# Moving the last wide-quarter products of a fused RWKV6 and MLP kernel into the kv burst

## The chip, the cores and the metric

The kernel runs on one core of a Trainium2 chip. The metric is the device time of one execution in microseconds (us). In the profile TensorE is PE (its weight loads PEld), VectorE is DVE, ScalarE is ACT, GpSimd is POOL and SyncE is SP. "L708" is line 708 of the kernel's source.

## The reference

Attention in the RWKV6 manner runs over 4 batches, 8 heads, 768 tokens and 48 channels; its result, 3072 tokens of 384 channels, goes through an MLP with an exact gelu.

```
for t in range(S):
    cur = einsum('bhd,bhe->bhde', u * k_t, v_t)
    y[:, :, t] = einsum('bhd,bhde->bhe', r_t, state + cur)
    state = w_t[..., None] * state + einsum('bhd,bhe->bhde', k_t, v_t)
x = y.transpose(0, 2, 1, 3).reshape(3072, 384)
h = x @ w_in                      # 384 x 2048
g = 0.5 * h * (1 + erf(h / sqrt(2)))
out = g @ w_out                   # 2048 x 384
```

## The kernel before, in words

The 3072 tokens are cut into 8 tiles of 384: tile x is one half of one batch's sequence, so odd tiles continue from the state that the tile before left. Within a tile the tokens form chunks of 64. Attention in a tile is computed by chunks: scores between the tokens of a chunk, the chunk's contribution k^T v to the state ("kv"), the chain of states from chunk to chunk, then outputs from inside the chunk and from the state before it.

**Order of work.** The work is written as generators, and one instruction stream per engine comes from stepping them in an order that a string fixes. `PLAN[x]` is the string of stage x: in it the MLP of tile x-1 and attention of tile x (and the start of that of tile x+1) are interleaved. Each character steps one stream: "." a group of MLP products on PE, "s" and "f" attention of this and the following tile, "x" sums that the MLP takes of its input (L1036), "v" merges of products (additions on DVE or by POOL transfers, L1115 to L1120), "g" gelus (L1133), "o" sums for and of the output products (L1161 to L1167), "e" copies of accumulators (L1084), "l" loads, and in the first stages "c", "w", "y", "p" for converting the weights and summing them. Nothing reorders this later: an engine runs its instructions in program order, each waiting for those that it depends on.

**The MLP.** Both products use fast multiplication: 20 products of half-blocks each, with sums and merges of inputs and outputs around them on DVE, ACT and POOL. Nearly all PE records of the MLP come from one line (L1040), each 128x128 weights by 192 columns, 0.1625 us apart.

**Attention of tiles 2 to 7** (`quarters()`, lines 661 to 782) makes the scores of a chunk in two levels: quarters of 4 tokens (FINE) and quarters of 16 ("wide"). For each level the 12 blocks of chunks are cut at 0, 5, 10 and 12. For each part `burst()` runs 64x64 products on PE (L708) into a pair of PSUM banks called d; there are two such pairs, and kv_ps and y_ps come from the same pool. Then `copy_quarters()` copies the scores into a_sb: on DVE under masks for the fine level (L737), on ACT in six copies for the wide level (L724, in `copy_rows`). The third part's burst therefore waits until the first part's copies have freed a pair. After the bursts DVE scales r and k for the next level (L753, L760, L764); at the wide level it transposes k in 32x32 blocks (L657), and 12 transfers on SP's queue (L652) and four ACT copies (L806) put the blocks of k^T in place.

Then, for the tile as a whole:

- kv burst on PE, 96 records into two pairs kv_ps, b = 0 and 1 (L822)
- chain of states on DVE, `chain_states()`: 20 multiply-adds (L837), and on even tiles two copies (L842) ahead of them
- `inside()`: 96 products within the chunks into two pairs y_ps (L863)
- `fences()`: a DVE copy of two columns of each y_ps pair (L875), which reads them and which the next products therefore have to wait for
- products with the states, added onto y_ps (L908)
- ACT copies of y_ps to the MLP's input xT (L931, L934) and six SP transfers (L938)

`halves()` does the same for tiles 0 and 1 with other levels. The planner's string decides which MLP products stand between these steps: in tiles 4 and 6 one group of them stood between `inside()` and the products with the states.

Of the kernel before, what the change touches and what calls it, by code (L numbers as in the profile page):

```python
# [10 lines left out]
F32 = mybir.dt.float32  # L11
# [10 lines left out]
C = 64  # L22
G = 64
D = 48
T = 384
# [3 lines left out]
NI = Q * N3  # L29
# [9 lines left out]
PLAN = {  # L39
    0: "l.s....llsl.lssslslss.lc.l.slslls...ssss..lcs.s.s.l.ss..ss..sccs.c.s.llpssslw..cs.ffpccxx",  # L40
    1: (
        "l.ccswccclss.cw.l.ccccccscs.c.csscccc.scc.sscwccc.cswcs.wcsccscccls.c.ssc.sclcswcwcc.wcwcc"
        "sslcw..cwlclwccswclsc.cf.w.cw..ccc.cfw..cfyx....f.x..x.f.yxxf.wxw..y..y...wywyx..xyxf.yw.f"
        ".wxywxyl.yf."
    ),
    2: (
        "s.w..s.w.w.s..w..wswv.w..v.ww.vwv.ssw.swgww.swgsvwv.w.sgwv.wssls..wvsw...wg...g...wvsw.gvl"
        "s..sgvss...gg.ssvgvw.wvgvgvv.glsgv..gs.og.l.oe.s.wsoeo.s...seooe..l.so.ooe.lewo...o..ooeoe"
        "..os.eolol.s.se..oo.oew.lsw.ooosles..f.fo.oo.o.fo..xooxxfxxxxxfxfxx"
    ),  # L50
    3: (
        ".ls....v..s.sl...g...s.vvs..s..l.vg.gvg....s..l..sv.svss.ssss.g.svssgvlvg.sg..vv.vv.gsv.gv"
        "s.sggv.gslsvs..g.ogsog.e..s.eoo.....seo.oe.os.eoo.e...oooso.e.e.s.soo.ool.lessseo..oeolssf"
        "....fooo.e..f.xooxo.o..x.oooxlxxxfxfxfxx"
    ),
    4: (
        "ls.....s.ss.v....g....vlv.s.gs.vv..g....sv...s.glssvvgsvslsss..gvs.v.gs.ggss..v.sgv.vv..vv"
        ".slsggs.svsg.gog.g.s.oss.eo.e.o..o.so..ee..ooo..eoe.o..oosee.s..loo.os.oes.e.so.llsleo.of."
        "s.o.esolo.f..f.ooo.o.foo..xoxxxxxxxffxfxx"
    ),  # L60
    5: (
        ".....sll....v....vv..vsg.vs....ggs.v..vs.ls..g.sv.ssssvs.sl..g.vs.vsvgs.s.ggv.gss..l..vsvv"
        "vsssvg...ggsggogsg.os.oe.se.l.o..o..o.oe.es.o.oeeo....o..ooseoes..ose.loos.ssell..oo.eossf"
        "..o..fo.oeof..o..xoo.oxox.oxxlxxxffxfxx"
    ),
    6: (
        "s..sl...v.....v..g..ss.v.lvv...g.gvs..gsv..s.v..s.ssggsssvss..ss.l.vg.s..vg.vvggss..vvvv.."
        "ssssvggg..g.so.ggsoe...seo...ssols.o.o.eooe...o.e.eo.o.o.e.ooeo..ssl.oos.lsel..eslooo..lef"
        "s..oes.o.lfo..foo.o.o..fooxoxxxxxffxxxfxx"
    ),  # L70
    7: (
        "....sv.......gss.v....vsv..g..sg..vvg..s...s.svsgvsvss.ss.ss.vvgs.v.gsg.vg..svg...vv.ssgsv"
        "v.gg.g.sgso.gseo..es.....osso..ooo.eeoo..e.eso...oooee...os.soe..oos.se.s.oeosos...oo.e..."
        "oooo..oxo.oxx.oxxxxxxxx"
    ),
    8: (
        "..........v...v...v.v..g.gggv.v.....vv.....g.gvg....vgv.vvvgvgv..vgg..g.vgo..gge..eo...o.o"
        ".oo.eoe....oeo.e.o..o.oeeo..oo.eo.o.eo....ooe..o.e.oo.o..o.oo.oo.o"
    ),
}  # L80

# [111 lines left out]
def kernel(  # L193
# [9 lines left out]
    nc = tc.nc  # L203
# [13 lines left out]
    wk = ctx.enter_context(tc.tile_pool(name="wk", bufs=2))  # L217
# [7 lines left out]
    def pair(name):  # L225
        return pools["d"].tile([128, 2, BANK], F32, name=name, tag="d")
# [22 lines left out]
    half = [slice(0, 64), slice(64, 128)]  # L249
# [8 lines left out]
    bufs = [io.tile([128, 3 * NP * T], F32, name=f"rkw{i}", bufs=1) for i in range(2)]  # L258
# [218 lines left out]
    def attention(x, unit):  # L477

        first = x % HALVES == 0
        parts = range(NPART) if units_of(x) == 1 else range(unit, unit + 1)  # L480
        np_ = len(parts)
# [179 lines left out]
        def quarters():  # L661
# [28 lines left out]
            for h in QUARTERS:  # L690
                m, r4, t4, s0, s1, s2 = views(h)

                def burst(first, behind):

                    d = pair("d")
                    if behind == n_b and h == FINE:
                        for a in range(FINE):
                            for g in range(2):
                                for p in range(2):
                                    nc.tensor.matmul(fine_of(d, g)[half[p], a * n_b:],  # L700
                                                     lhsT=places[half[g], a, p * C:(p + 1) * C],
                                                     rhs=fine_sb[half[g], 0:FINE - a, a],
                                                     start=(a == 0), stop=True, skip_group_check=True)
                    for n in range(first, behind):
                        i = n - first
                        for g in range(2):
                            for p in range(2):
                                nc.tensor.matmul(d[half[p], g, i * 3 * C // 2:(i + 1) * 3 * C // 2],  # L708
                                                 lhsT=kc[half[g], n // NI, n % NI, p],
                                                 rhs=rx[half[g], 2 * n + p], start=True, stop=True,  # L710
                                                 skip_group_check=True)
                    return d
# [27 lines left out]
                last = h == QUARTERS[-1]  # L740
# [75 lines left out]
        kvs = []  # L816
        for b in range(np_):
            kv_ps = pair("kv_ps")
            for i in range(NI):
                for p in range(2):  # L820
                    for g in range(2):
                        nc.tensor.matmul(kv_ps[half[g], p, i * D:(i + 1) * D], lhsT=k_t(b, i, p, g),  # L822
                                         rhs=vs(b, i, g)[half[p], 0:D], start=True, stop=True)
# [28 lines left out]
        def inside():  # L852

            for b in range(np_):
                if split:
                    y = [bank("y_ps") for _ in range(2)]
                else:
                    y_ps = pair("y_ps")
                    y = [y_ps[:, c] for c in range(2)]
                for i in range(NI):  # L860
                    for p in range(2):
                        for g in range(2):
                            nc.tensor.matmul(y[p][half[g ^ swap(b)], i * C:(i + 1) * C], lhsT=vs(b, i, g)[half[p]],  # L863
                                             rhs=at[half[p], g, b * NI + i, :], start=(i == 0), stop=True, skip_group_check=True)
                ys.append((y, None if split else y_ps))

        def fences():

            for y, y_ps in ys:
                fence = wk.tile([128, 2], F32, name="fence")  # L870
                if split:
                    for c in range(2):
                        nc.vector.tensor_copy(out=fence[:, c:c + 1], in_=y[c][:, NI * C - 1:NI * C])
                else:
                    nc.vector.tensor_copy(out=fence, in_=y_ps[:, :, NI * C - 1])  # L875

        if x == 0:

            inside()
            yield  # L880
            for z in last_r:
                z()
            yield
            chain_states(range(NC - 1 + int(first)))
            yield
            fences()
            yield
        else:
            for c in range(0, NC, 2):
                chain_states(range(c, min(c + 2, NC - 1 + int(first))))  # L890
                if x > 1 and c + 2 < NC:
                    yield
            yield
            inside()
            fences()
            yield

        for i in range(NI):
            for p in range(2):
                for b in range(np_):  # L900
                    q, c3 = divmod(i, N3)
                    for g in range(2):
                        c = 2 * c3 + (p + g) % 2
                        src, c0 = (st, c - 1) if c else (before, NC - 1)
                        if src is None:
                            continue
                        o = ((parts[b] * Q + q) * NC + c0) * D
                        nc.tensor.matmul(ys[b][0][c % 2][half[g ^ swap(b)], i * C:(i + 1) * C],  # L908
                                         lhsT=src[half[g], o:o + G], rhs=rc[half[g], b, i, c % 2],
                                         start=False, stop=True, skip_group_check=True)  # L910
# [415 lines left out]
```

## Time and profile before

| what | us |
|---|---|
| three runs | 580.93, 584.48, 581.96 (median 581.96) |
| the profiled execution | 584.98 |
| its span | 583.2 |
| PE busy | 557.0 (96%) |
| DVE busy | 491.9 (84%) |
| ACT busy | 330.3 (57%) |
| POOL busy | 103.1 (18%) |
| transfers on SP's queue and others | 25.6% of 16 engines' span |
| transfers by POOL | 20.0% of 16 engines' span |

The span is the time from the first to the last instruction that the profiler saw; the execution's own time is a little longer. Busy time is the union of an engine's instructions, with modelled ends for matmuls. In a line of the timeline the columns are start, duration of the group, engine, source line, operation, output<-input, tile, size and count; the bracket at the end is idle time of that engine just ahead, and what ended it. In the list of waits the three numbers are summed idle time, how often, and the longest.

### The profile page before, as it was taken

The page shows a single profiled execution, that of the slowest core. Times are in us where ns is not written, and L with a number is a line of the kernel's source. Part 1 is how long each engine was busy: PE and PEld are TensorE (multiplying, and loading weights), DVE is VectorE, ACT ScalarE, POOL GpSimd, SP SyncE. Part 2 cuts the span into 40 slices and gives each one's busy share as a digit, 9 for nine tenths or more (in the row PEclk, how much of TensorE's full clock was granted, in tenths as well). Part 3 has the DMA queues.
Part 4 walks back from the last instruction along what each step waited for, and adds up shares of the span by engine and source line. Part 5 has one row for each costly group of instructions (what it writes and reads, how often), then busy time and mean ns, then how long its engine had stood idle before and what let it go on. Part 6 is the DMA issues. An engine that isn't in the chain of part 4 may idle for free. (4 is left out here: it accounts for less than half of the span.)

```text
span 583.2 us, 17698 instructions
## 1 busy us (share of the span) xinstructions
PE 557.0 (96%) x7410; PEld 492.4 (84%) x7424; DVE 491.9 (84%) x997; ACT 330.3 (57%) x733; POOL 103.1 (18%) x99
## 2 busy tenths in 40 slices
PE   6889999999999999999999999999999999999997
PEld 3675666579998988998898998999998988989997
DVE  6988979998989989799988988799888988855464
ACT  2368998027852575537763566527772568525820
POOL 3200000005400370005400352005500172000000
PEclk9999999999999999999999999999999999999999
DMA  7749850038633692337822693328814493201001
GB/s 244 214 127 365 305 204 12 28 111 115 80 77 104 148 160 31 90 97 151 116 37 80 177 141 43 79 75 174 111 27 126 108 118 47 41 14 42 0 1 40
DMA packets 71646, 62.15 MB, mean 107 GB/s; under 512 B 32912, under 2 KB 56720, under 8 KB 71568
## 3 DMA queue, kind: packets, MB, share of 16 engines
q1 hardware_dynamic: 50256, 45.62, 25.6%
q0 software_dynamic: 21216, 15.34, 20.0%
q8 instruction: 58, 0.95, 0.7%
q14 instruction: 20, 0.16, 0.1%
q10 hardware_dynamic: 96, 0.07, 0.1%
HBM read 36.24 MB, written 4.72 MB: 70 GB/s over the span
## 5 line engine op out<-in xcount | busy, mean ns | idle before, releaser
L1115 POOL DMA_DIRECT2D g<-o_sb x78 | 95.1, 1504 | 373.5 <-ACT g L1084 273.0
L1164 DVE TENSOR_TENSOR g<-g 128x512 f32<-128x512 f32 x112 | 75.1, 687 | 20.4 <-PE o_ps L1040 17.2
L1040 PE MATMUL h_ps<-forms_x,w_in_sb 128*128 128x192 f32 x280 | 58.2, 333 | 1.2 <-ACT g L1084 0.7
L1084 ACT COPY o_sb<-u_ps 128x384 f32<-128x384 f32 (+1 forms) x56 | 25.6, 458 | 54.0 <-PE u_ps L1040 52.5
L1040 PEld LDWEIGHTS h_ps<-forms_x,w_in_sb 128*128 128x128 f32 x280 | 46.2, 190 | 5.0 <-ACT g L1084 2.9
L1040 PE MATMUL o_ps<-w_out_sb,g 128*128 128x192 f32 x280 | 50.2, 326 | 0.0
L1084 ACT COPY g<-h_ps 128x384 f32<-128x384 f32 x84 | 40.1, 479 | 16.0 <-PE h_ps L1040 13.9
L1133 ACT ACTIVATE g<-g 128x384 f32<-128x384 f32 x98 | 46.4, 519 | 3.7 <-DMA g<-o_sb 2.6
L1040 PEld LDWEIGHTS o_ps<-w_out_sb,g 128*128 128x128 f32 x280 | 46.2, 190 | 0.3 <-ACT g L1133 0.3
L1040 PE MATMUL o_ps<-t,g 128*128 128x192 f32 x224 | 41.5, 328 | 0.2 <-DVE g L1120 0.2
L724 ACT COPY a_sb<-d 32x320 f32<-32x320 f32 (+5 forms) x108 | 39.1, 362 | 4.1 <-PE h_ps L1040 1.5
L1040 PEld LDWEIGHTS o_ps<-t,g 128*128 128x128 f32 x224 | 36.7, 190 | 1.1 <-DVE g L1120 0.5
L1040 PE MATMUL h_ps<-forms_x,s 128*128 128x192 f32 x168 | 35.9, 336 | 0.5 <-ACT u_ps L1084 0.3
L1051 PE MATMUL h_ps<-xT,w_in_sb 128*128 128x384 f32 x96 | 34.0, 497 | 1.2 <-ACT g L1053 1.0
L1040 PE MATMUL h_ps<-xT,w_in_sb 128*128 128x192 f32 x168 | 34.8, 330 | 0.0
L708 PE MATMUL d<-kx,rkw 64*64 64x96 f32 x1152 | 31.6, 248 | 2.5 <-ACT a_sb L724 1.5
L708 PEld LDWEIGHTS d<-kx,rkw 64*64 64x64 f32 x1152 | 25.5, 133 | 8.9 <-issue 3.8
L1040 PE MATMUL u_ps<-xT,w_in_sb 128*128 128x192 f32 x168 | 32.1, 327 | 0.1
L1040 PE MATMUL u_ps<-w_out_sb,g 128*128 128x192 f32 x168 | 31.3, 333 | 0.5 <-ACT u_ps L1084 0.5
L1059 PE MATMUL o_ps<-w_out_sb,g 128*128 128x384 f32 x96 | 31.4, 488 | 0.0
L573 PEld LDWEIGHTS d<-rkw 64*64 64x64 f32 x1152 | 20.3, 141 | 13.1 <-issue 7.1
L1040 PEld LDWEIGHTS h_ps<-forms_x,s 128*128 128x128 f32 x168 | 27.5, 189 | 4.1 <-ACT u_ps L1084 3.6
(169 smaller groups left out, 1199.3 us busy)
## 6 DMA issues: line engine op xcount, KB each, us to landing
g<-o_sb POOLq DMA_DIRECT2D x78, 192.0 KB, 4.2
rkw<-in_rkw_dram SPq DMA_DIRECT2D x54, 256.0 KB, 4.4
raw<-in_w_out_dram SPq DMA_DIRECT2D x8, 768.0 KB, 5.1
v_in<-in_v_dram SPq DMA_DIRECT2D x8, 584.0 KB, 4.0
out_dram<-o_sb SPq DMA_DIRECT2D x24, 192.0 KB, 1.9
raw<-in_w_in_dram SPq DMA_DIRECT2D x5, 768.0 KB, 10.3
rkw<-kx SPq DMA_DIRECT2D x72, 48.0 KB, 2.0
rkw<-in_rkw_dram SPq DMA_DIRECT2D x6, 384.0 KB, 6.6
```

The lines of the kernel that those rows point to most:

```text
L573: nc.tensor.matmul(d[half[p], g, n * width:(n + 1) * width], lhsT=kc[half[g], b, i, p], rhs=right(half[g], b, i, p), start=True, stop=True)
L708: nc.tensor.matmul(d[half[p], g, i * 3 * C // 2:(i + 1) * 3 * C // 2], lhsT=kc[half[g], n // NI, n % NI, p], rhs=rx[half[g], 2 * n + p], s ...
L724: nc.scalar.copy(out=at[z, g, first:behind, (a + 1) * h:], in_=d[z, :, :, to] if g == slice(None) else d[z, :, to])
L1040: nc.tensor.matmul(o, lhsT=lhsT, rhs=rhs, start=start, stop=True, skip_group_check=True)
L1051: nc.tensor.matmul(h_ps, lhsT=w_in_sb[:, f // FI, j, f % FI * 128:(f % FI + 1) * 128], rhs=xT[:, j, :], start=(j == 0), stop=(j == NJ - 1))
L1059: nc.tensor.matmul(o, lhsT=gs[f // FG][:, f % FG, i * 128:(i + 1) * 128], rhs=w_out_sb[:, f, :], start=(f == 0), stop=(f == NF - 1))
L1084: nc.scalar.copy(out=o, in_=z)
L1115: nc.gpsimd.dma_start(out=o, in_=saved[q, t], accum_op=ALU.add)
L1133: nc.scalar.activation(out=o, in_=z, func=AF.Gelu, scale=MINUS.get(h, 1.0))
L1164: nc.vector.tensor_add(o, o, g_block(what[3:5]))
```

## The change

1. For the wide level of tiles 2 to 7 the third part (two blocks, 8 products of which PE records 16) is put off. ACT copies the two blocks of k into a buffer `kept` before k is scaled further, and the products run at the head of the kv burst, into columns of kv_ps of b = 0 behind those that kv uses (`NI*D` on). Their six ACT copies come right after the kv burst.
2. The fences of all tiles but tile 0 go from DVE to ACT.
3. A step ends ahead of `inside()` and none between the fences and the products with the states, so that these always stand together on PE. The products with the states run over b in the outermost loop.
4. The strings PLAN[1] to PLAN[8] are written anew; PLAN[0] stays.

```diff
-                def burst(first, behind):
-
-                    d = pair("d")
+                def burst(first, behind, d=None, kn=None):
+
+                    d = pair("d") if d is None else d
...
-                                                 lhsT=kc[half[g], n // NI, n % NI, p],
+                                                 lhsT=kn(half[g], n, p) if kn else kc[half[g], n // NI, n % NI, p],
...
-                ds.append(burst(*parts_of[2]))
+                if last:
+
+                    a, b = parts_of[2]
+                    kept = wk.tile([128, T], F32, name="ysb", bufs=1)
+                    nc.scalar.copy(out=kept[:, 0:(b - a) * 128], in_=k[:, a * 128:b * 128])
+
+                    def left(d, a=a, b=b, burst=burst, copy_quarters=copy_quarters, kept=kept):
+                        d = d[:, :, NI * D:]
+                        burst(a, b, d, lambda z, n, p: kept[z, (n - a) * 128 + p * C:(n - a) * 128 + (p + 1) * C])
+                        return lambda: copy_quarters(a, b, d)
+
+                    late.append(left)
+                else:
+                    ds.append(burst(*parts_of[2]))
...
-        last_r = []
+        last_r, late = [], []
...
             kv_ps = pair("kv_ps")
+            if b == 0:
+                late = [z(kv_ps) for z in late]
...
             kvs.append(kv_ps[:, :, 0:NI * D].rearrange("p c (q i e) -> p q i c e", q=Q, e=D))
+        for z in late:
+            z()
         yield
...
-                    nc.vector.tensor_copy(out=fence, in_=y_ps[:, :, NI * C - 1])
+                    (nc.vector.tensor_copy if x == 0 else nc.scalar.copy)(out=fence, in_=y_ps[:, :, NI * C - 1])
...
             yield
+            yield
             inside()
             fences()
-            yield
-
-        for i in range(NI):
-            for p in range(2):
-                for b in range(np_):
+
+        for b in range(np_):
+            for i in range(NI):
+                for p in range(2):
```

In the new source the lines of this part are L708 (bursts), L724 (copies), L753 (the copy into `kept`), L773 and L777 (scaling of k), L837 (kv burst), L854 and L859 (states), L880 (inside), L892 (fences), L925 (products with states), L1040 becomes L1057, L1084 L1101, L1167 L1184.

More of the change, by code (lines that the diff above doesn't have):

```diff
@@ L41 @@
     1: (
-        "l.ccswccclss.cw.l.ccccccscs.c.csscccc.scc.sscwccc.cswcs.wcsccscccls.c.ssc.sclcswcwcc.wcwcc"
-        "sslcw..cwlclwccswclsc.cf.w.cw..ccc.cfw..cfyx....f.x..x.f.yxxf.wxw..y..y...wywyx..xyxf.yw.f"
-        ".wxywxyl.yf."
-    ),
-    2: (
-        "s.w..s.w.w.s..w..wswv.w..v.ww.vwv.ssw.swgww.swgsvwv.w.sgwv.wssls..wvsw...wg...g...wvsw.gvl"
-        "s..sgvss...gg.ssvgvw.wvgvgvv.glsgv..gs.og.l.oe.s.wsoeo.s...seooe..l.so.ooe.lewo...o..ooeoe"
-        "..os.eolol.s.se..oo.oew.lsw.ooosles..f.fo.oo.o.fo..xooxxfxxxxxfxfxx"
-    ),
@@ L61 @@
-    5: (
-        ".....sll....v....vv..vsg.vs....ggs.v..vs.ls..g.sv.ssssvs.sl..g.vs.vsvgs.s.ggv.gss..l..vsvv"
-        "vsssvg...ggsggogsg.os.oe.se.l.o..o..o.oe.es.o.oeeo....o..ooseoes..ose.loos.ssell..oo.eossf"
-        "..o..fo.oeof..o..xoo.oxox.oxxlxxxffxfxx"
-    ),
-    6: (
-        "s..sl...v.....v..g..ss.v.lvv...g.gvs..gsv..s.v..s.ssggsssvss..ss.l.vg.s..vg.vvggss..vvvv.."
-        "ssssvggg..g.so.ggsoe...seo...ssols.o.o.eooe...o.e.eo.o.o.e.ooeo..ssl.oos.lsel..eslooo..lef"
-        "s..oes.o.lfo..foo.o.o..fooxoxxxxxffxxxfxx"
-    ),
@@ L71 @@
-    7: (
-        "....sv.......gss.v....vsv..g..sg..vvg..s...s.svsgvsvss.ss.ss.vvgs.v.gsg.vg..svg...vv.ssgsv"
-        "v.gg.g.sgso.gseo..es.....osso..ooo.eeoo..e.eso...oooee...os.soe..oos.se.s.oeosos...oo.e..."
-        "oooo..oxo.oxx.oxxxxxxxx"
-    ),
-    8: (
-        "..........v...v...v.v..g.gggv.v.....vv.....g.gvg....vgv.vvvgvgv..vgg..g.vgo..gge..eo...o.o"
-        ".oo.eoe....oeo.e.o..o.oeeo..oo.eo.o.eo....ooe..o.e.oo.o..o.oo.oo.o"
+        "sc.cc.sc.lsscccc.wwccccssw.sccc.wlcsclccclscw.ssc.ccsccsc.ssccc.sc.cslwsswcc.ccc.lwccscclw"
@@ new lines @@
+        "s.wcllcsc.ww.fscc....cf.fcwlcccwcw.cwfwccwx..w...fxxcc.yx..wyyy.yxwx..yy.xxy..xy..fy.yffw."
+        "..w.x.x.f..."
+    ),
+    2: (
+        ".ws..wwsw...s..wv.w.w...sv.w.wvw.slwsw.vgww.gsv.w.s.swvsg.w.wswws..g..vwg.s..gw.v.gvs...gv"
+        "sw.g.vssvwgsswsw.vgsvvv.lgg.v.llgsvgs..o.ge..osw.eo...so.o..o.oseoeo..eo.eswl...ooel..oeo."
+        "o.soo..el.selsso.lo.o.fseso...fw.e.ooof.o..oosox.o.oxxxfxxxxwflxfxx"
+    ),
+    3: (
+        "s...l.s.s....vs..v......vgs..gsvv.vg....vv.s.g.g..vs.vslsglssg.ss.sss..vv..s..vgsvv.gsvgss"
+        ".sgvs..vgggsg.lgoos.s..eos..eo...o..oooee.o..e..leoo..se..oooes..so.leo.lo.eslls.ssoeoo.sf"
+        "..f.oo.oef.o..o.o..ooxoxl.xoxxxxsfxfxfxxf"
+    ),
@@ new lines @@
+    4: (
+        "....v.ss......v....vs.vs..sglg...gg.v..s..v.gs.lssssv..vsssv.l.sv.gsvsv.g.g.svv.v.vs.sg.lv"
+        ".gs.gvgsggs.gsgo.leo.s.lsoe...o.s.o.oo.ee..o.oo..eooe.os...ee..soso.e.oloel.s.sso.es.losof"
+        "..o.es..f.oo...ofoooo.oxofxlxxxxfxxxfxx"
+    ),
+    5: (
+        "....lv...lss.....vv...g....gs.v.g.vsvv.ls.s.sv...v.s.sgsssvssgs.v.gg..svs.ggg..svs.sv.ssgv"
+        "l.svgv.gsvs.go.g.g.eo..esso.s...ooso...oeeo.lo.eo.loe...oee.oso.o..soolse.s..es.o.oellofss"
+        "..fo..s.oeo.o.foox.ox..loxo.oxxxxxffxfxx"
+    ),
@@ new lines @@
+    6: (
+        ".sls..........s.v..v.vvs.gl..v.sglsv..g...s.g..sg.svsss..s.v.v.vg.lvg.s.vs.vgg.slsgssvsv.."
+        "ssgvvvg.sss.gg.googss.e.s.e.o..o...eoooe..o.o...eoe.solo...eooeo..ss.olo.el.e.sssosl.o.eof"
+        "s.o.foe.o..fol.o.so.o.o.oxoxxxxxfxxfxfxx"
+    ),
+    7: (
+        "........vs..v....s.vvvg...s.v.vvgg...g..ssssgv....vs.ssgs.svs.sv.sg.ggs.s.vs.sgvvvs..sssv."
+        ".gsv..ggggs.g.eo.ose.s.s.osos...oeoooe..o..oe.o.eo..o.e.oeo..s.ooses.e..so.oeoss...oo.eo.."
+        "o.oo..ox..oooxxxxxsxxxxx"
+    ),
@@ L79 @@
+    8: (
+        "......v.......gvgv....v.vv...g..v..gv...g.g..v..g.v..g.vvg.vvg.vvggv.g..vg.g.go..eeoo....."
+        "o.o..oeoeo.o.o.eoo.e..oe..oe..oo.eo...e..ooeo.o..o.e.o.ooo...ooo.o"
     ),
```

6 lines of the change are left out of this document (removed).

## The prediction

> **What bounds the kernel now.** I read the page's busy shares and slices, then the list of waits, then the timelines of TensorE (PE) and VectorE (DVE) around one tile, then busy time by stretch.
>
> ```profile
> PE 557.0 (96%) x7410; PEld 492.4 (84%) x7424; DVE 491.9 (84%) x997; ACT 330.3 (57%) x733; POOL 103.1 (18%) x99
> PEclk9999999999999999999999999999999999999999
> ```
>
> PE is busy for 96% of the span at full granted clock, so a gain must come from PE's few gaps or from fewer records. The waits that the change aims at are small:
>
> ```profile
> PEld y_ps L908 <- DVE fence L875: 3.8, 7, 1.1
> PE d L708 <- ACT a_sb L724: 1.5, 4, 0.4
> PE y_ps L908 <- issue: 1.5, 2, 0.8
> ```
>
> I cut tiles 2 to 7 at two places that the PE timeline shows: the kv burst (L822) and the first quarter burst after it (first L708 x40). The kv bursts start at 174.24, 241.26, 307.63, 375.26, 441.51, 509.44; the quarter bursts of tiles 3 to 7 at 210.35, 276.83, 342.80, 410.48, 477.28. So "first stretches" (kv to next quarters) last 36.11, 35.57, 35.17, 35.22, 35.77, and "second stretches" (quarters to kv) 30.91, 30.80, 32.46, 31.03, 32.16. Busy time, in the order PE, PEld, DVE, ACT, POOL, of one of each:
>
> ```profile
> 442.00:476.00 34.00, 32.89 (x433) 31.06 (x434) 32.33 (x74) 16.37 (x37) 9.37 (x8) 1.00 0.54 122
> 411.00:441.00 30.00, 29.61 (x357) 27.78 (x349) 26.38 (x43) 20.19 (x52) 5.75 (x5) 1.00 0.43 61
> ```
>
> In the first stretch DVE is as full as PE, and it delivers what the quarters need (L684). Its start and end there:
>
> ```profile
> 442.89 0.26 DVE L842 COPY st<-kv_ps 128x96 f32<-128x96 f32 x1 [0.31 <-PE kv_ps L822]
> 443.59 0.26 DVE L842 COPY st<-kv_ps 128x96 f32<-128x96 f32 x1 [0.44 <-PE kv_ps L822]
> 443.76 3.58 DVE L837 SCALAR_TENSOR_TENSOR st<-st,tot_sb,kv_ps 128x48 f32<-128x48 f32 x20
> 451.26 0.21 DVE L875 COPY fence<-y_ps 128x2 f32<-128x2 f32 x2
> 476.17 0.96 DVE L684 TENSOR_TENSOR kx<-kx,tot_sb 128x768 f32<-128x768 f32 x1 [0.66 <-ACT kx L678]
> ```
>
> The states begin 1.38 after the kv burst started; between them and L684 DVE has hardly an idle moment. So a delay of the states moves the next quarters by as much. In the second stretch DVE has air (26.38 of 30) and PE leads. PE's places that change, tiles 6 and 7:
>
> ```profile
> 441.51 2.04 PE L822 MATMUL kv_ps<-v_in,rkw 64*64 64x48 f32 x96
> 447.58 1.63 PE L863 MATMUL y_ps<-a_sb,v_in 64*64 64x64 f32 x96
> 449.14 1.57 PE L1040 MATMUL o_ps<-t,g 128*128 128x192 f32 x8
> 451.51 1.41 PE L908 MATMUL y_ps<-rkw,st 64*64 64x64 f32 x80 [0.80 <-DVE fence L875]
> 490.29 1.06 PE L708 MATMUL d<-kx,rkw 64*64 64x96 f32 x40
> 491.73 0.56 PE L708 MATMUL d<-kx,rkw 64*64 64x96 f32 x16 [0.39 <-ACT a_sb L724]
> 518.73 0.34 PE L908 MATMUL y_ps<-rkw,st 64*64 64x64 f32 x6 [0.78 <-issue]
> ```
>
> **The change part by part.** *Fewer bursts.* By the order of the built programs PE has 60 bursts of 64x64 products before and 55 after (one less in tiles 2, 4 and 6, two less in 3). Entering a burst costs .10 over the .1625 of a 128x192 product, leaving it .15 (gap .17 against .02), its first large record another .10: .35 each, 1.75 in all. This pays only where PE leads.
>
> By the Trainium skill, "TensorEngine Tiling (Array Packing)", section Key Properties, a change of tiling mode drains TensorE; the gaps above agree, and by that rule alone the sum would be 581.96 - 1.75 = 580.2, which lies inside the forecast's own range.
>
> *The stall at the wide quarters' third burst.* It stands right behind the second and waits for ScalarE's L724 to free a pair: .60 between products in each of tiles 4 to 7. The edit removes it; in its place comes one ScalarE copy of 128x256 (L753 after), bounded by L724's smallest form below (16x64, 0.204) and the 128x384 copies above (L1084, 0.458); I take 0.35, nearer to the upper row by its size. DVE's product at L773 must wait for it, but reaches it .9 later than ScalarE ends it (15.7 against 14.8 after the first quarter burst), so it costs nothing; without that cover, 0.35 per tile. The gelus queued behind it on ScalarE shift: the first output product, which waits for them, comes at 17.35 instead of 17.88 since six L724 copies (1.63) left this place.
>
> *Second stretch, sum.* PE then needs about 30.4 (30.6 in tile 5). The 12 SP transfers of L652 bound it below: transposes end, 8 us of issue, 2.0 of landing, four copies: 30.1. Taken against each old length: -.5, -.4, -1.9, -.6, -1.7 = -5.1. Tiles 5 and 7 lose more since there PE also waited 1.6 for POOL's merge (L1120), which the new slots place later. Bounds: 0 (the gelus are late as before) and -6.6 (at the transfers' bound).
>
> *Kv burst and the states: what the change adds.* Late results lie in kv_ps of b=0, and their six copies follow the whole kv burst. The built order has the wait that follows from it, in tiles 2, 5, 6, 7:
>
> ```
> 273 L859 TensorCopy st_134<-kv_ps 128x2x48 [waits PE_49,Activation_49]
> 558 L854 TensorScalarPtr st_135<-st_134,tot_sb,kv_ps 128x48 [waits PE_49,Activation_49]
> 652 L859 TensorCopy st_134<-kv_ps 128x2x48 [waits PE_49,Activation_49]
> 748 L854 TensorScalarPtr st_135<-st_134,tot_sb,kv_ps 128x48 [waits PE_49,Activation_49]
> ```
>
> ScalarE's count there is that of the last of the six copies: DVE may not read kv_ps before. In tiles 3 and 4 the same wait sits one step earlier, at L1184 (o_sb<-o_sb,o_ps), which needs a ScalarE copy queued behind the six. So the states start, after the burst's start: 16 records x .0207 = .33, 48 x .0149 = .715, .26 latency, six copies 1.63 (the group of 32x128, 16x192, 16x64 at 504.77), .04 = 2.98; in tiles 3 and 4 with one more ScalarE copy and L1184 3.6. Before it was .99, 1.01, 1.01, 1.01, 1.38. Behind the wait on DVE stand the 20 steps and then the sums L1164 and L1167, which PE's next output products read; behind the six copies on ScalarE stand copies of output sums (L1084). The wait could cost 0 (if DVE had slack) to its full 2 to 2.6; I take it in full, since DVE's idle time in this stretch is .5 to 1. What goes out: the idle before the second half of kv_ps (.47, .26, .44, .26, .44) and the fences with their waits (.53, .62, .13, .87, .13). Tile by tile: 2.98-.99-.47-.53 = +.99; 3.6-1.01-.26-.62 = +1.71; 3.6-1.01-.44-.13 = +2.02; 2.98-1.01-.26-.87 = +.84; 2.98-1.38-.44-.13 = +1.03. Sum +6.6. Behind the states PE's products inside chunks wait for DVE's last state (their banks are kv's), .6 to 1.5 per tile; it is the same delay, not a second one.
>
> A rule speaks against the change: the Trainium skill, "PSUM — Partial Sum Buffer", section "PSUM bank collisions raise a hardware error", says that two engines, readers too, must not use one bank and quadrant at a time, and that the compiler orders such pairs. No row of before shows such a pair; the built order above does.
>
> *Fences on ScalarE.* Before, DVE's fence could stand behind four L512 (3.04 us, tiles 4 and 6), and PE waited .80. Now ScalarE copies b=0's while PE runs b=1's products inside chunks (done at +.99, copy .2, PE busy to +1.43): hidden; uncovered it costs .2 to .4. SP's queue keeps its L652 and L938 issues in their order.
>
> *Start and end.* Up to the first kv burst: one burst less in tile 2 (-.35), and tile 1's fence wait of .64 between the two bursts, of which I take .5: -.85 (within 1.5 either way, since stage 1 is full on ScalarE too and its slots are new). From the last kv burst to the end: 16 records +.33, products inside waiting for the states +.9, fence -.40, half of the .97 issue stall -.48: +.35.
>
> *Sum:* +6.6 - 5.1 - .85 + .35 = +1.0. The profiled execution took 584.98 (span 583.2, 1.78 around it), 3.02 over the median of 581.96; it goes to 586.0, the median to 583.0.
>
> **The rivals.** *Faster:* the states' delay is not on the path, because DVE makes it up elsewhere. Then 581.96 - 5.1 - .85 + .35 = 576.4. For it: 30 us of DVE work lie between, part of it (L1036, L1167) waiting for other engines. Against: DVE is 95% busy there, and its instructions between states and L684 are the same but for two fences.
>
> *Slower:* the second stretch doesn't shorten, since its output products still wait for gelus that the kept copy and merges push back. Then 581.96 + 6.6 - .85 + .35 = 588.1. It decides if the first output product comes later than 17.9 after the quarter burst, as before. Against: six copies have left ScalarE ahead of it.
>
> That the change does nothing is excluded by the built order: 55 bursts.
>
> **How the numbers follow.** About 1% is what a measurement of this kernel can tell from no change. Forecast (+1.0, own range 578.5 to 586): .64; faster rival .20; slower rival .16. Low 576.0 and high 588.0 leave out the outer half of each rival. The chances of faster, same, slower are these three.
>
> **What would show it.** Right: "DVE st <- ACT a_sb L724" of about 1.7 in four tiles, DVE L1184 waiting about 2.6 for ScalarE in tiles 3 and 4; PE's L880 waiting for DVE's st; no L708 waiting for L724; fence waits near 0; first stretches 37.1, 37.3, 37.2, 36.1, 36.8, second ones 30.4 to 30.6. Wrong: first stretches as before (the faster rival), second ones of 31 to 32 (the slower), or a start up to the first kv burst off by more than 1.5.

## The result, and the profile after

The changed kernel takes 600.45 us against 582.32 before: ratio 1.0291, 95% interval 1.0255 to 1.0327. The forecast of 583.0 and its range (576.0 to 588.0) are missed on the slow side. The profiled execution took 599.50 with a span of 597.7 (before: 583.2), 0.95 below its median; that of before, 584.98, lies 2.66 above its own. So the two profiles differ by 14.5, the medians by 18.1, and what follows explains the 14.5.

The page of the changed kernel, busy time by engine:

```profile
PE 567.9 (95%) x7424; PEld 500.3 (84%) x7424; DVE 490.2 (82%) x983; ACT 335.6 (56%) x753; POOL 102.9 (17%) x99
PEclk9999999999999999999999999999999999999999
```

PE loads as many weights as before (PEld, x7424) but is busy 10.9 longer at the same clock: some of its products became slower. The list of waits of the changed kernel (us in all, times, longest):

```profile
DVE o_sb L1184 <- ACT o_sb L1101: 5.8, 2, 3.0
DVE st L859 <- ACT a_sb L724: 4.6, 2, 2.3
DVE st L854 <- ACT a_sb L724: 4.5, 2, 2.2
PE y_ps L880 <- DVE st L854: 4.3, 6, 1.0
PE y_ps L925 <- issue: 2.3, 3, 1.0
```

The predicted wait is there: DVE's states stand behind the late copies, 2.2 to 2.3 in tiles 2, 5, 6 and 7 (1.7 forecast), and 2.9 by way of L1184 in tiles 3 and 4 (2.6). Gone are PE's waits at L708 for L724 and most of those for fences. Cut at the same two places as in the prediction (with the late products counted as the head of the kv burst):

| us | before | after | forecast change | measured change |
|---|---|---|---|---|
| start to the first kv burst | 174.24 | 174.39 | -.85 | +.15 |
| five first stretches | 177.83 | 192.73 | +6.6 | +14.9 |
| five second stretches | 157.37 | 155.06 | -5.1 | -2.3 |
| last kv burst to the end | 73.75 | 75.54 | +.35 | +1.8 |

The first stretches can be cut once more, at DVE's first state and at L684, which delivers what the next quarters need; from L684 to the quarter burst it is 1.11 in all of them, before and after.

| us | tile 2 | 3 | 4 | 5 | 6 | sum |
|---|---|---|---|---|---|---|
| burst's first record to the states, before | .99 | 1.01 | 1.01 | 1.01 | 1.38 | 5.4 |
| the same, after | 3.29 | 3.92 | 4.03 | 3.29 | 3.40 | 17.9 |
| states to L684, before | 34.01 | 33.45 | 33.05 | 33.10 | 33.28 | 166.9 |
| the same, after | 35.14 | 32.85 | 34.85 | 32.84 | 33.59 | 169.3 |

So 12.5 of the 14.9 is the later start of the states. Tile 4's first stretch grew most (35.17 to 39.99). ScalarE, then DVE, in the changed kernel there:

```profile
315.37 1.63 ACT L724 COPY a_sb<-kv_ps 32x128 f32<-32x128 f32 x6 [1.33 <-PE kv_ps L837]
317.02 0.32 ACT L1101 COPY o_sb<-o_ps 128x192 f32<-128x192 f32 x1
```

```profile
317.37 0.35 DVE L1184 TENSOR_TENSOR o_sb<-o_sb,o_ps 128x192 f32<-128x192 f32 x1 [2.96 <-ACT o_sb L1101]
317.64 0.42 DVE L859 COPY st<-kv_ps 128x96 f32<-128x96 f32 x2
317.97 3.58 DVE L854 SCALAR_TENSOR_TENSOR st<-st,tot_sb,kv_ps 128x48 f32<-128x48 f32 x20
...
327.94 1.42 DVE L1181 TENSOR_TENSOR g<-g 128x512 f32<-128x512 f32 x2 [0.45 <-PE o_ps L1057]
...
331.72 0.37 DVE L1178 TENSOR_TENSOR u_ps<-u_ps,o_sb 128x192 f32<-128x192 f32 x1 [0.65 <-PE u_ps L1057]
...
334.32 0.35 DVE L1184 TENSOR_TENSOR o_sb<-o_sb,o_ps 128x192 f32<-128x192 f32 x1 [0.41 <-PE o_ps L1057]
```

The states begin 4.03 after the burst's first record (317.64 - 313.61). In this tile a second loss follows: DVE, which once the states had begun waited for no such product before, now waits for PE's output products, 1.5 in the three waits of these lines and .22 in a fourth. PE's side of it:

```profile
321.35 1.63 PE L880 MATMUL y_ps<-a_sb,v_in 64*64 64x64 f32 x96 [0.70 <-DVE st L854]
322.77 1.03 PE L925 MATMUL y_ps<-rkw,st 64*64 64x64 f32 x29
324.85 1.55 PE L925 MATMUL y_ps<-rkw,st 64*64 64x64 f32 x51 [1.04 <-issue]
326.33 1.57 PE L1057 MATMUL o_ps<-t,g 128*128 128x192 f32 x8
```

PE waits for the states, then runs 176 small products at once, and in the middle stands 1.04 with no wait that the profile shows; only then do output products come that DVE needs. This loss is not in every tile: DVE's waits for PE's output products add up to 2.0 and 1.7 in tiles 2 and 4, where PE so stands, and to .2, .2 and .6 in tiles 3, 5 and 6, where PE waits for the states as well (L880, .5 to 1.0) but doesn't stand. Tile 6 has the third loss in one line, to be held against 451.51 of before (80 products with the states in 1.41):

```profile
461.17 2.37 PE L925 MATMUL y_ps<-rkw,st 64*64 64x64 f32 x80
```

Between starts, in tile 5, four records took 58 to 59 ns before (6, 7, 7, 38), and two do now (52, 6).

### The profile page after: what moved, and what is told of

Same layout as the page of the kernel before. It is cut to its first block, busy times and chain, and to the rows that moved or that the text cites. A ratio compares the mean times of both kernels' runs of the same rounds, so it can differ in the third digit from the quotient of the medians.

```text
span 597.7 us, 17696 instructions
## 1 busy us (share of the span) xinstructions
PE 567.9 (95%) x7424; PEld 500.3 (84%) x7424; DVE 490.2 (82%) x983; ACT 335.6 (56%) x753; POOL 102.9 (17%) x99
## 4 chain that ended last, share of the span: by engine, by line
PE 64%; DVE 14%; ACT 14%; issue 5%; DMA 1%; SPq 0%; ACTq 0%; DVEq 0%
PE u_ps L1057 17%; PE o_ps L1057 15%; PE h_ps L1057 14%; PE o_ps L1076 5%; ACT a_sb L724 4%; DVE st L854 3%; PE y_ps L925 3%; DVE a_sb L737 3%; ACT xT L948 2%; PE y_ps L880 2%; PE d L573 2%; PE d L708 2%; ACT g L1150 2%; PE kv_ps L837 1%; DVE a_sb L795 1%
## 5 line engine op out<-in xcount | busy, mean ns | idle before, releaser
L1057 PE MATMUL h_ps<-forms_x,w_in_sb 128*128 128x192 f32 x280 | 58.2, 333 | 0.6 <-ACT g L1101 0.5
L1101 ACT COPY o_sb<-u_ps 128x384 f32<-128x384 f32 (+1 forms) x56 | 25.7, 459 | 54.5 <-PE u_ps L1057 53.4
L1057 PE MATMUL o_ps<-w_out_sb,g 128*128 128x192 f32 x280 | 51.2, 330 | 0.5 <-DVE o_sb L1184 0.5
L1057 PEld LDWEIGHTS h_ps<-forms_x,w_in_sb 128*128 128x128 f32 x280 | 46.3, 190 | 4.5 <-ACT g L1101 3.6
L1057 PEld LDWEIGHTS o_ps<-w_out_sb,g 128*128 128x128 f32 x280 | 45.6, 190 | 3.3 <-ACT g L1150 1.5
L1101 ACT COPY g<-h_ps 128x384 f32<-128x384 f32 x84 | 40.1, 480 | 13.1 <-PE h_ps L1057 11.0
L1057 PE MATMUL o_ps<-t,g 128*128 128x192 f32 x224 | 43.1, 332 | 1.8 <-DVE g L1137 0.8
L1057 PEld LDWEIGHTS o_ps<-t,g 128*128 128x128 f32 x224 | 36.6, 190 | 4.7 <-ACT g L1150 2.5
L1057 PE MATMUL h_ps<-forms_x,s 128*128 128x192 f32 x168 | 35.6, 335 | 0.0
L1057 PE MATMUL u_ps<-w_out_sb,g 128*128 128x192 f32 x168 | 31.8, 333 | 3.5 <-ACT u_ps L1101 3.5
L1057 PE MATMUL h_ps<-xT,w_in_sb 128*128 128x192 f32 x168 | 34.8, 330 | 0.0
L724 ACT COPY a_sb<-d 32x320 f32<-32x320 f32 (+2 forms) x72 | 29.9, 416 | 6.6 <-DVE a_sb L795 5.3
L854 DVE SCALAR_TENSOR_TENSOR st<-st,tot_sb,kv_ps 128x48 f32<-128x48 f32 x160 | 28.8, 257 | 4.5 <-ACT a_sb L724 4.5
L1057 PE MATMUL u_ps<-xT,w_in_sb 128*128 128x192 f32 x168 | 32.1, 327 | 0.0
L1057 PEld LDWEIGHTS u_ps<-w_out_sb,g 128*128 128x128 f32 x168 | 27.2, 190 | 5.6 <-ACT u_ps L1101 5.3
L573 PEld LDWEIGHTS d<-rkw 64*64 64x64 f32 x1152 | 19.6, 139 | 14.5 <-issue 8.0
L708 PE MATMUL d<-kx,rkw 64*64 64x96 f32 x1056 | 28.3, 247 | 2.1 <-DVE a_sb L795 1.4
```

Of the source, the lines that this page charges most:

```text
L573: nc.tensor.matmul(d[half[p], g, n * width:(n + 1) * width], lhsT=kc[half[g], b, i, p], rhs=right(half[g], b, i, p), start=True, stop=True)
L724: nc.scalar.copy(out=at[z, g, first:behind, (a + 1) * h:], in_=d[z, :, :, to] if g == slice(None) else d[z, :, to])
L854: nc.vector.scalar_tensor_tensor(out=stq[:, q, c], in0=stq[:, q, c - 1] if c else b4[:, q, NC - 1], scalar=totq[:, q, c:c + 1], in1=kvs[q ...
L1057: nc.tensor.matmul(o, lhsT=lhsT, rhs=rhs, start=start, stop=True, skip_group_check=True)
L1101: nc.scalar.copy(out=o, in_=z)
```

## The experiments

Ratios are to the kernel before, with 95% intervals; "P", "S", "H", "R" and "X" name theories in the expectations. The changed kernel is 1.0291 [1.0255, 1.0327].

**The loop order**, undone in the changed kernel (e1) and made alone (e2):

```diff
-        for b in range(np_):
-            for i in range(NI):
-                for p in range(2):
+        for i in range(NI):
+            for p in range(2):
+                for b in range(np_):
```

> The changed kernel with the old loop order of the products with the states (b innermost but for g), all else as changed. Theory P (pace): in the trace of after these products alternate between two of PE's four 64x64 positions, 58 ns for two records, where before four records took 59 ns; so the burst is 1.0 to 1.2 us longer in each of tiles 1 to 7, some 8 in all. P expects the burst back at 1.2 to 1.5 us and the kernel at 592 to 595 (some of the 8 is given back, since both fences are now ahead of the first four records). Rival S (states): the loss comes from the states that wait for ScalarE's late copies; PE would only wait longer ahead of the next quarters, so 599 to 601.

> The kernel before with only the new loop order of the products with the states (b outermost). P expects these bursts at 2.1 to 2.7 us and the kernel at 588 to 590. S expects 582 to 583.5, since nothing that DVE waits for has changed.

e1: 597.91, 1.0234 [1.0192, 1.0276]. e2: 585.66, 1.0055 [1.0020, 1.0090]. Products with the states, groups by form, first of the kernel before, then of e2:

```profile
L908 PE MATMUL y_ps<-rkw,st 64*64 64x64 f32 x704 | 15.2, 221 | 4.5 <-DVE fence L875 2.4 <-issue 1.5 <-DVE fence L873 0.5
```

```profile
L908 PE MATMUL y_ps<-rkw,st 64*64 64x64 f32 x704 | 21.7, 220 | 2.7 <-DVE fence L875 2.0 <-DVE fence L873 0.5 <-issue 0.2
```

The order makes these products 6.5 us slower, but costs the kernel only about 3 either way (0.55 to 0.57% of 582). Of the two runs e2 shows it: its interval leaves out 1, while that of e1 overlaps with the changed kernel's. Part of the slower burst stands where PE waited before (the idle time ahead of these products falls from 4.5 to 2.7); where the rest goes was not followed. P is right about the pace and wrong about the price; S is wrong that it costs nothing. In e1's profile the five first stretches add up to 191.77, so the order makes 1.0 of the 14.9 there.

**Late burst undone, and new slots alone.** e3 takes the third burst back to its old place in the changed kernel; e10 puts the new strings into the kernel before.

> The changed kernel with the wide quarters' third burst put back to its old place (no kept copy, no late copies behind kv), the new loop order and slots stay. S expects most of the 18 back: 584 to 589. P expects only the states' share of the delay, 3 to 7: 593.5 to 597.5. In both no DVE state waits for ScalarE's L724.

> The kernel before with the new slot strings PLAN[1] to PLAN[8] and nothing else changed in the code. P and S both put the loss elsewhere and expect 581 to 585. A third theory, L, holds the new slots themselves to be worse for the chip, and expects 587 or more.

e3: 655.55, e10: 656.55. Neither answers: with the third burst in its old place a tile has one step more (its copies), so, by the count of steps, under the new strings attention's last step came after the MLP's sums of x, which then read an earlier tile's values. e3b and e5b let two copies share a step.

```diff
                 for z, d in list(zip(parts_of, ds))[1:]:
                     copy_quarters(*z, d)
-                    yield
+                    if not (last and z == parts_of[1]):
+                        yield
```

> The changed kernel with the wide quarters' third burst back at its old place, and the steps counted so that the slots fall as they do in the changed kernel (two copies of scores share one step). The new loop order, one burst, ACT fences and new slots stay. Theory H: the late copies hold DVE's states back by 2 to 3 us per tile, PE then stands ahead of its products inside chunks, and DVE afterwards waits for PE's output products, so the late burst alone costs 12 to 14: expects 585 to 589. Rival R (burst and slots): the late burst costs no more than the 7 of the prediction, and the rest comes from the slow and stalled burst of products with states and from the new slots: expects 594 to 597.

> As the run before, and with the old loop order of the products with states. H expects 583 to 586; R, with the order worth 2.5 us as the first runs gave it, expects 591 to 595.

e3b: 600.69, 1.0312 [1.0271, 1.0353]; e5b: 600.28, 1.0299 [1.0260, 1.0337]. Without the late burst the new slots are as slow as with it, against H, and for another reason than R's: PE waits at the third burst for ScalarE's copies, up to 1.9 at a time (before, up to 0.4), and second stretches grow by 6.7 in sum, to 32.5 and 35.5. That is not all: the start to the first kv burst is 5.6 longer in e5b, and first stretches 4.1. The waits of e5b:

```profile
PE d L708 <- ACT a_sb L724: 4.8, 4, 1.9
```

The strings are made for a kernel with the late burst; these runs tell nothing of its price. One thing can be read from e5b's first stretches: its states start 1.0 to 1.4 after the kv burst, as before, and still DVE then waits 3.5 for PE's products up to L684 (before .85, at its fences). These waits don't need late states. To price the late burst it has to be put into the old slots:

**The late burst alone** in the kernel before, with an empty step in place of the copies' one (e11); the same with the six copies issued behind the states (e12); the same without the copies (f1).

The edit of e12 against e11 (f1 has only the first part of it):

```diff
-        for z in late:
-            z()
         yield
...
                     yield
+            for z in late:
+                z()
             yield
             inside()
```

> The kernel before with the late burst alone (kept copy, products at the head of the kv burst, copies behind it; an empty step keeps the slots where they were); DVE fences, old order, old slots. H expects 592 to 597, with DVE's first state waiting about 2 us for ScalarE's L724 in each of tiles 2 to 7. R expects 583 to 589.

> The late burst alone in the kernel before, but its six ScalarE copies are issued behind DVE's chain of states, so that DVE reads kv_ps first and ScalarE waits for DVE. The same work on every engine as in the run with the late burst alone (597.2). Theory H (DVE is held back): the states start 1.0 to 1.4 after the kv burst's 96 records as before, first stretches return to 35 to 36.5, and the time to 585 to 589; PE waits up to 2 us ahead of its products inside chunks. Rival X (the work itself costs: kept copy, the 16 records ahead of kv, six more copies at a busy place of ScalarE): 593 or more.

> The late burst alone in the kernel before, with its six ScalarE copies left out: the scores of two of twelve blocks are then those of an earlier tile, so the output is not the reference's. Kept copy and late products stay. Theory H2 (the copies are the whole cause, by DVE's wait and by ScalarE's queue): 583 to 587. Rival X (records and kept copy): 591 or more.

e11: 597.24, 1.0244 [1.0196, 1.0292]. e12: 592.95, 1.0162 [1.0105, 1.0219]. f1: 588.23, 1.0095 [1.0064, 1.0127]. H holds for e11: the late burst alone makes most of the loss. Its five first stretches grow by 9.9 (177.83 to 187.75), its second ones by 0.2, the end by 2.3. The states start 12.6 later in sum, as in the changed kernel, but the way from them to L684 is 2.7 shorter than before, and DVE's waits for PE's products on it stay at .8. DVE in tile 4 of e11, then of f1:

```profile
316.42 0.42 DVE L861 COPY st<-kv_ps 128x96 f32<-128x96 f32 x2 [2.33 <-ACT a_sb L724]
```

```profile
312.90 0.26 DVE L859 COPY st<-kv_ps 128x96 f32<-128x96 f32 x1 [0.80 <-PE kv_ps L839]
313.60 0.26 DVE L859 COPY st<-kv_ps 128x96 f32<-128x96 f32 x1 [0.44 <-PE kv_ps L839]
```

e12 fell between H and X. Tile 5 of e12 shows why:

```profile
384.27 1.63 ACT L724 COPY a_sb<-kv_ps 32x128 f32<-32x128 f32 x6 [4.98 <-DVE st L854]
385.93 0.32 ACT L1103 COPY o_sb<-u_ps 128x192 f32<-128x192 f32 x1
386.28 0.36 DVE L1180 TENSOR_TENSOR u_ps<-u_ps,o_sb 128x192 f32<-128x192 f32 x1 [1.75 <-ACT o_sb L1103]
386.30 0.92 PE L1059 MATMUL u_ps<-t,g 128*128 128x192 f32 x4 [2.25 <-ACT o_sb L1103]
```

Now ScalarE waits for DVE, and an output copy queued behind the six makes both DVE and PE wait. The states of e12 start 9.4 sooner in sum than those of e11, but the way from them to L684 is 7.5 longer. In percent of the kernel, the late burst's 2.4 split into about 0.8 that goes when DVE reads first, 0.7 more when the copies go, and 0.95 that stays without them: records ahead of kv, the kept copy and whatever shifts with them, not told apart further. By the intervals the first two are known to about 0.7 only.

**The other parts alone:** fences on ScalarE from tile 1 (e7) or tile 2 on (e13), one burst (e6), and both (g2).

```diff
-                    nc.vector.tensor_copy(out=fence, in_=y_ps[:, :, NI * C - 1])
+                    (nc.vector.tensor_copy if x < 2 else nc.scalar.copy)(out=fence, in_=y_ps[:, :, NI * C - 1])
```

> The kernel before with only the fences of tiles 1 to 7 on ScalarE. If DVE sets the first stretches, DVE's waits at the fences (.53, .62, .13, .87, .13 in tiles 2 to 6) come back: 580 to 581. If ScalarE's queue is busy at that moment, or DVE's time there isn't on the path: 582 to 584.

> The kernel before with the fences of tiles 2 to 7 on ScalarE, those of tiles 0 and 1 on DVE. In the run with all of tiles 1 to 7 on ScalarE (585.0) PE stood 2.77 us ahead of tile 1's products with the states, since the fence stood behind weight conversions (.64 before), and both kinds of stretches were 3.3 us shorter in sum. If those are two separate effects: 580.5 to 582.5. If the shorter stretches only made up for the late start: 583.5 to 585.

> The kernel before with the products inside chunks put in the same step as those with the states (old order, old slots, DVE fences). If a burst saved is worth its .35 of switching: 581.5 to 583.5. If 192 records back to back outrun PE's supply of instructions (PE stood 1.0 us without a wait in such bursts of tiles 2 and 4 of the changed kernel) and both fences are now in the open: 584 to 587.

> The kernel before with the fences on ScalarE from tile 2 on and the products inside chunks in one step with those with the states; old order, old slots, no late burst. If the two parts' shorter stretches add up: 578.5 to 581.5. If they remove the same wait twice: 581.5 to 584.

e7: 585.04, 1.0035 [1.0008, 1.0062]. In tile 1 ScalarE converts weights, and the fence stands behind them; PE of e7, then of before:

```profile
95.20 1.65 PE L908 MATMUL y_ps<-rkw,st 64*64 64x64 f32 x96 [2.55 <-ACT fence L875]
```

```profile
92.12 1.68 PE L908 MATMUL y_ps<-rkw,st 64*64 64x64 f32 x96 [0.42 <-DVE fence L875]
```

e13, without that (its edit is the diff above; e7 has `x == 0` for `x < 2`), took 582.14, 0.9979 [0.9954, 1.0004]: the fastest kernel here, but its interval includes no change (1). e6, which moves a `yield` from behind the fences to ahead of `inside()`: 585.36, 1.0026 [0.9997, 1.0056]; g2: 585.03, 1.0010 [0.9988, 1.0033]. One burst gains nothing measurable. In e6's profile the joined bursts of tiles 4 and 6 run without PE standing in them; the two places where it stands with no wait shown are in tiles 2 and 7, as before (.60 and .66; before .73 and .78).

**All of it, with the copies out of DVE's way** (e15: old order, late products in b = 1's pair, copies behind the states), and **the old slots** (f8: the changed kernel with old order and old strings):

> The changed kernel with three things undone or moved: old loop order, the late products in kv_ps of b=1, their copies behind the states (products inside chunks of b=0 need not wait for them). New slots, one burst and ACT fences stay. H expects the order's 3 and most of the late burst's 10 in first stretches back: 585 to 589. If the new slots by themselves cost as much as the late burst, whatever DVE does: 592 to 596.

> The changed kernel with the old slot strings (an empty step keeps their count) and the old loop order; late burst, one burst and ScalarE's fences stay. The same with the new slots took 597.9. If the new slots help the late burst as they are made for it: 599 to 602. If they cost by themselves: 593 to 596.

e15: 592.34, 1.0154 [1.0102, 1.0207], .8% below e1, as e12 is below e11. f8: 600.11, 1.0278 [1.0227, 1.0329] against e1's 1.0234 [1.0192, 1.0276]: the new slots may help the late burst by 2 to 3 us, which these intervals don't settle. In the profiles f8's first stretches (189.51) are 2.3 shorter than e1's, its second ones (157.28) 2.2 longer.

**What sets the second stretch.** Transposes, transfers, kv burst in tile 5, before and after:

```profile
362.98 1.95 DVE L657 STREAM_TRANSPOSE kx<-rkw 128x384 f32<-128x384 f32 x4
365.08 8.00 SPq L652 DMA_DIRECT2D rkw<-kx  x12
...
375.26 1.67 PE L822 MATMUL kv_ps<-v_in,rkw 64*64 64x48 f32 x96
```

```profile
372.38 1.96 DVE L657 STREAM_TRANSPOSE kx<-rkw 128x384 f32<-128x384 f32 x4
...
374.49 8.01 SPq L652 DMA_DIRECT2D rkw<-kx  x12
...
384.34 0.56 PE L708 MATMUL kv_ps<-kx,ysb 64*64 64x96 f32 x16
```

From the transposes' end (364.93, 374.34) to the burst it is 10.33 and 10.00. In all five tiles it is 10.2 to 10.4 before; after, 10.0 in four and 10.7 in the last. So the stretch is as long as DVE makes it up to the transposes, plus ten. DVE has little idle time there: 1.26 ahead of the first scores in every tile, 1.67 and 1.55 more ahead of a merge (L1120) in tiles 5 and 7 of before, and otherwise at most .22. PE, whose stall at the third burst is gone, now waits for ScalarE's gelus ahead of the output products' weight loads; the list of waits before, then after:

```profile
PEld o_ps L1040 <- ACT g L1133: 0.3, 1, 0.3
```

```profile
PEld o_ps L1057 <- ACT g L1150: 4.0, 10, 0.6
```

f3 and f4 tried to shorten the ten by issuing two or four transfers on ScalarE's queue (on top of e13; f4 has `i % 2 == 1`):

```diff
-            for move in moves[:NC_SP]:
-                move_block(nc.sync, *move)
+            for i, move in enumerate(moves[:NC_SP]):
+                move_block(nc.scalar if i % 3 == 2 else nc.sync, *move)
```

> The kernel before with ScalarE's fences from tile 2 on, and two of the twelve transfers of k's blocks issued on ScalarE's queue. If the chain of transposes, transfers (8.0 us of issue, 2.0 of landing) and kv burst sets the second stretches, they get up to 1.3 shorter until PE's own work binds: 577 to 581. If PE binds them already: 581.5 to 583.

> As the run before with four of the twelve on ScalarE's queue. If the chain sets the stretches: 575 to 581. If ScalarE's gelus and copies queued behind the transfers (which wait for the transposes) come late: 583 to 588.

f3: 602.10, 1.0312 [1.0267, 1.0358]; f4: 615.09, 1.0534 [1.0464, 1.0604]. They made the link longer instead. In f3 ScalarE's queue reaches its two transfers before the transposes are done, stands 4.63 in all (1.29 of it to issue them), and the copies behind them come late; the kv burst starts when the last L806 ends:

```profile
372.58 1.29 ACTq L652 DMA_DIRECT2D rkw<-kx  x2
372.65 6.84 SPq L652 DMA_DIRECT2D rkw<-kx  x10
373.92 0.32 ACT L1084 COPY o_sb<-o_ps 128x192 f32<-128x192 f32 x1 [4.63 <-issue]
...
385.98 2.08 ACT L806 COPY rkw<-kx 32x384 f32<-32x384 f32 x4
388.04 1.66 PE L822 MATMUL kv_ps<-v_in,rkw 64*64 64x48 f32 x96
```

From the transposes' end to the burst it is 11.4 to 15.5, and f3's second stretches are 17.3 longer in sum, as much as its span (17.2). So a late k block is paid for in full, while what an earlier one would bring stays open.

**Why the new order is slow** (g1: i, b, p). With b outermost the products of one pair stand at two of PE's 64x64 positions in turn; with b inside, at four.

> The kernel before with the products with the states in the order i, b, p (before it was i, p, b; the changed kernel has b, i, p). Position theory: a record waits for the one before it at the same 64x64 position of PE, so with (0,0) and (1,1) twice and then (0,1) and (1,0) twice, about one pair in two waits: 92-record stretches take 1.8 to 2.3 us, between the 1.4 of before and the 2.6 of the changed kernel. Bank theory (the pace falls since one pair of banks is written all through the burst): banks change every four records, so 1.4 to 1.5 as before.

g1: 584.08, 0.9998 [0.9967, 1.0028]; its products are busy for 16.5 (15.2 before, 21.7 in e2). It doesn't tell the theories apart after all: while two products wait for the first two positions, the next two run at the others, which gives four records in about 58 ns by either theory, and my expectation missed that. What speaks for positions is `inside()`: it stays on one pair of banks for 48 records, goes over four positions, and keeps the fast pace (four records in 58 ns, 1.41 from the first start to the last of 96). That the pace halves with two positions in turn is shown; that a position has to finish first is the likeliest reason, not a shown one.

## Why the prediction was wrong, point by point

- **The loop order had no term.** The prediction named it neither as a cost nor as a rival, though the diff shows it. It made the products with the states 6.5 slower (e2 against before) and costs about 3 us. Leaving these products at their old pace was the mistake: an edit that changes only the order of PE's products still needs a price.
- **"Kv burst and the states", +6.6: right in mechanism, wrong in what goes out.** The wait was found in the built order and came as said. The sum has two parts. The later start of the states is +10.7 in it and was +12.5; in tile 4 the six copies begin 1.76 after the burst's first record, where the sum has 1.31. The idle and the fences that go out are -4.15, and this is the step that failed: it takes them in full, as if no other wait could come in their place. In the runs the way from the states to L684 became 2.4 longer. DVE was busy on it for 157.8 against 158.3, but its waits for PE's products there rose from .85, at the fences, to 4.8, none at a fence. They don't come from the delay handed back by PE: in e11 the states are as late and these waits don't grow, so "it is the same delay, not a second one" holds there, and 2.7 of the credit came; in e5b the states aren't late, and the waits are 3.5. They come with the rest of the change, for which the prediction had no term: first stretches grow by 9.9 with the late burst alone (e11), 11.7 with one burst and ScalarE's fences (f8), 13.9 with the new slots (e1) and 14.9 with the new order. Each is one profile, and why PE's output products come late for DVE is not settled; where PE stood in the joined burst (tiles 2 and 4) it was worst.
- **"Second stretch, sum", -5.1: the step failed.** It took PE and the gelus for what sets this stretch and put 30.1 as the transfers' bound. In the runs kv follows the transposes by ten us, and DVE reaches them no sooner for a PE stall of .60 removed: e11 has that stall removed and its second stretches change by +0.2. In the changed kernel PE's stall moved more than it went, to waits for gelus (the two lines above f3). The -2.3 of the changed kernel is mostly tile 5 (32.46 to 30.74), where the transposes start earlier (from 20.18 to 18.78 after the quarter burst) since DVE's wait of 1.67 for a merge is gone. The new slots need not be the reason: with the old ones e2 has 31.06 there and e6 31.08, with .28 and .30 of that wait, and e11 32.39 and e13 32.16 with 1.60 and 1.38. The kept copy was not free: it took .39 to .41 (.35 forecast), and DVE waited for it three times, 1.0 in all. That the third burst's stall cost nothing could have been read from before: tile 3 without it had 30.91, tiles 4 and 6 with it 30.80 and 31.03.
- **"Fewer bursts", 1.75.** Not to be seen: one burst alone (e6) is 1.0026 [0.9997, 1.0056]. In the changed kernel PE stood 1.0 to 1.04 without a shown wait in the middle of the joined bursts of tiles 2 and 4. A load of 16,384 bytes on the instruction queue, the trace shows, started at 183.06 and at 322.26, 2.3 and 2.6 ahead of PE's going on. In the traces of before, e1 and e6 too, each such stop of .5 or more in these bursts ended 2.3 to 2.8 after such a load had started, though not each load brings a stop. That the products outran their instructions fits this, and was not tested; that joined bursts alone bring it about is not so, since before has two such stops and e6 has no more. The drain that the Trainium skill ("TensorEngine Tiling (Array Packing)", section Key Properties) states remains as the rows of before have it, 0.35 a burst; no run shows that saving it moves the end.
- **Fences on ScalarE: hidden in tiles 2 to 7,** as said (e13 is no slower). In tile 1 the old slots would have cost 2.1 more (2.55 against 0.42), which the new slots avoid.
- **Start and end.** The start moved by +.15 against -.85, within the stated 1.5; the first quarter burst, up to which e11 and f1 are the kernel before, came 1.2 and 2.3 later in their profiled executions, so such a size tells nothing. The end took +1.8 against +.35; with the late burst alone it is +2.3 (e11), where the states' wait has little behind it to hide it.
- **The rivals.** The faster one didn't come: first stretches grew. The slower one gave 588.1 by the second stretch not shortening, and in e11 it doesn't; but first stretches were then 3 to 8 more than it had. Its mechanism, output products that wait for gelus, is in the same two lines; its sign was a poor one, since the products o_ps<-w_out_sb start 17.5 to 17.8 after the quarter burst, not later than 17.9, and the stretch stays long because the transposes set it. The order between two engines at one bank, for which the Trainium skill ("PSUM — Partial Sum Buffer", section "PSUM bank collisions raise a hardware error") was cited against the change, agrees with the trace: 2.2 to 3.0 of waiting in each of six tiles.

## What to carry to other kernels

Putting results into spare columns of a PSUM bank that another engine is about to read ties two engines together: ask who reads that bank next and whether that reader is on the path. Before counting a stall that goes as a gain, follow what the next burst waits for; here the kv burst waited for a chain behind DVE, and PE's stall ahead of it cost nothing. And when engines run in fixed program order, an idle time that an edit removes is a gain only if no other wait takes its place: here 4.15 us of such credits were counted, and the same way became 2.4 longer.

## What the runs showed of the hardware

- 64x64 products at two positions in turn take 58 ns for two records, at four positions 58 ns for four (bursts of 80: 2.37 and 1.41 us).
- Two transfers on ScalarE's queue, which had to wait for VectorE's transposes, held that queue for 4.63 us in tile 5, 1.29 of it to issue them; the copies behind them came late enough to make the kernel 3.1% slower (f3).
- Ten stops of PE of .5 to 1.4 us inside 64x64 bursts, with no wait shown, ended 2.3 to 2.8 us after a 16,384-byte load on the instruction queue had started (before, after, e1, e6); cause not tested.
